# Linear attention into a gated feed-forward block on one core: batch 0's exponentials row by row on ScalarE, two more maximum trees, chunk 0 in halves, and a new written-out order

## The chip, the core and the metric

The kernel runs on one core of a Trainium2 chip. Its engines run side by side: TensorE (PE in the profile, its weight loads PEld) multiplies matrices, VectorE (DVE) and ScalarE (ACT) work on elements, GpSimd (POOL) does slower element work and issues some of the loads, SyncE (SP) issues the other loads and all stores. The metric is the device time of the whole program in microseconds: before the change the median of three runs is 242.53 us, between 241.72 and 242.69.

## What is computed

`q`, `k`, `v` have the shape 8 batches x 8 heads x 576 rows x 64, in float32. The feed-forward part has 4608 tokens (8 x 576) of width 512 and an inner width of 1024.

```python
q_s = softmax of q over the 64 features of a row          # + 1e-09 in the sum
k_s = softmax of k over the 576 rows, for each feature    # + 1e-09 in the sum
kv  = k_s^T @ v                 # 64 x 64 for each batch and head
x   = q_s @ kv                  # laid out as 4608 x 512
a, b = x @ w1, x @ w2           # 4608 x 1024 each
out = (a * b @ w3) @ w_out      # 4608 x 512, float32
```

## The kernel before

**Folding the weights.** `w3 @ w_out` is computed once, because the second part is linear after `a * b`. For each of eight slices `ft` of 128 rows of `w3`, step `w3t.ft` transposes the slice on PE (L416), `w3T.ft` copies it out of PSUM, `pf.ft.0` and `pf.ft.1` (L428) multiply it with the two halves of `w_out`, and `W3O.ft` scales it out. The loads are named `w3.0` to `w3.5` (the last two, `w3.4` and `w3.5`, hold two slices each: slices 4, 5 and 6, 7) and `wo.0`, `wo.1`.

**Attention of a batch `b`.** The 576 rows of a head lie as 64 partitions x 9 rows, two groups of heads fill the 128 partitions.
- For `k`: `kmx` is the maximum over the 9 rows that a partition holds. Batches below `TREES` (L285, two of them) take it as a tree of four `tensor_tensor` maxima over the whole tile (L469 to L472); the others as two `tensor_reduce` over half of the heads each (L460). `cb` (L474 to L488) brings it over the partitions: a transpose, reductions, a transpose back. `ksub` subtracts (L491), `kexp` takes the exponential on ScalarE (L499), `kv` multiplies with `v` on PE (L516, L526), `kv2` divides by the sum (L535 to L538).
- For `q`, in two parts (part 0 has 4, part 1 has 5 of a partition's 9 rows for each head): `qmx` maximum (L545), `qsub` subtraction (L550), `qexp` one exponential over the part (L558), `qsm` sum of each row (L563), `qeps` and `qrc` the reciprocal (L569, L575), `qn` the product (L582). Then `q` is transposed: on PE for batches 0 and 1 (`qt` L597, copied by `qT`), with a transposing DMA (`qd`) afterwards.
- `xm` and `xt` (L630) form `x` transposed, `xs` and `xts` scale it into SBUF as float16.

**Feed-forward of a chunk `c`.** Chunks 0 to 7 are 512 tokens of a batch each; chunk 8 gathers the last 64 tokens of all batches. For each slice `u`, `up.1` and `up.0` multiply with `w2` and `w1` (L744), `bs` copies the first out of PSUM, `ab` multiplies the two on VectorE (L759). `down.c.tb` (L766) sums eight matmuls, one for each slice of `ab`, for 128 tokens; `os` copies, `st` stores. A chunk in `SPLIT` (L294, chunk 1) is done in two halves of 256 tokens, named `sub` 0 and 1: a step `up.1.c.sub.u` then does two slices for half of the tokens. `down.c.0` reads the last `ab` of its half only in its last matmul, or in its last two where the chunk is split (two slices each).

**What sets the order.** All steps are written out in one list, `ORDER` (L80). Each engine gets its steps in that order and runs them strictly one after the other, so a step that waits holds up everything that is behind it on its engine. `PICKS` says which engine takes a step that two can do. `FILL` puts matmuls on zeros in front (17 at the start, 16 ahead of `pf.4.0`); nobody uses their result. For the first `LINKED` = 191 steps a step that holds the SBUF port that VectorE and GpSimd share waits for the last such step of the other engine (L71 to L75). `HW` (L193) are the loads that SyncE issues first, `LOADS` (L198) those of GpSimd; a GpSimd load also waits for the load eight places ahead of it to land (L401). The later loads are issued by SyncE, in the order of `ORDER`.

Of the kernel before, what the change touches and what calls it, by code (L numbers as in the profile page):

```python
# [17 lines left out]
class Plan:  # L18
# [8 lines left out]
    @staticmethod  # L27
    def group(name):

        if name[0] == "cast":  # L30
            return "_".join(str(x) for x in name)
        return f"{name[0]}_{min(name[1], 3)}_" + "_".join(str(x) for x in name[2:])
# [57 lines left out]
qT.1.0 up.1.0.0.3 ksub.1.0 ab.0.0.2 up.0.0.0.3 bs.0.0.3 kmx.2.1 kexp.1.1 xt.0 up.1.0.0.4 xts.0.1  # L90
up.0.0.0.4 xts.0.0 q.1.1 kexp.1.0 ab.0.0.3 up.1.0.0.5 cb.2 up.0.0.0.5 bs.0.0.5 bs.0.0.4 kv.1 q.2
W3O.6 v.2 ab.0.0.4 k.3 ksub.2.1 up.1.0.0.6 kv2.1 up.0.0.0.6 bs.0.0.6 ab.0.0.5 xm.1.0 up.1.0.0.7
ab.0.0.6 xs.1.0.0 ksub.2.0 xs.1.0.1 kexp.2.1 up.0.0.0.7 qmx.1.1 up.1.1.0.0 bs.0.0.7 up.0.1.0.0
ab.0.0.7 qsub.1.1 kexp.2.0 qmx.2.1 up.1.1.0.1 bs.1.0.0 up.0.1.0.1 bs.1.0.1 ab.1.0.0 up.1.1.0.2
qsub.2.1 qexp.1.1 qmx.2.0 down.0.0 q.3 qsm.1.1 v.3 vc.2.1 up.0.1.0.2 qexp.2.1 ab.1.0.1 up.1.1.0.3
vc.2.0 bs.1.0.2 qeps.1.1 os.0.0 up.0.1.0.3 qrc.1.1 bs.1.0.3 qsm.2.1 st.0.0 qn.1.1 kv.2 down.0.1
k.4 kv2.2 ab.1.0.2 qsub.2.0 qt.1.16 qt.1.8 ab.1.0.3 qT.1.16 down.0.2 qT.1.8 os.0.1 qmx.3.1
qexp.2.0 xm.1.1 down.0.3 xs.1.1.1 q.4 qsm.2.0 qsub.3.1 qeps.2.1 xs.1.1.0 qmx.3.0 os.0.2
up.1.1.1.0 os.0.3 up.0.1.1.0 qrc.2.1 bs.1.1.0 st.0.3 kmx.3.1 qn.2.1 qeps.2.0 xt.1 up.1.1.1.1
qexp.3.1 up.0.1.1.1 bs.1.1.1 qrc.2.0 qsm.3.1 down.1.0 xts.1.0 qn.2.0 qd.2.1 vc.3.1 ab.1.1.0  # L100
st.0.1 qeps.3.1 up.1.1.1.2 xts.1.1 qsub.3.0 qmx.4.1 qd.2.0 up.0.1.1.2 bs.1.1.2 vc.3.0 up.1.1.1.3
ab.1.1.1 qsub.4.1 v.4 ab.1.1.2 down.1.1 st.0.2 qexp.3.0 kmx.3.0 bs.1.1.3 up.0.1.1.3 os.1.0 os.1.1
st.1.0 xm.2.0 ab.1.1.3 down.1.2 xs.2.0.0 qrc.3.1 st.1.1 xs.2.0.1 cb.3 qn.3.1 xm.2.1 down.1.3
xs.2.1.1 xs.2.1.0 qsm.3.0 ksub.3.1 qd.3.1 qexp.4.1 up.1.2.0.0 kmx.4.0 up.0.2.0.0 bs.2.0.0 os.1.3
up.1.2.0.1 ksub.3.0 qeps.3.0 ab.2.0.0 up.0.2.0.1 bs.2.0.1 qsm.4.1 kexp.3.1 up.1.2.0.2 up.0.2.0.2
bs.2.0.2 qrc.3.0 ab.2.0.1 qn.3.0 kexp.3.0 up.1.2.0.3 ab.2.0.2 up.0.2.0.3 kmx.4.1 bs.2.0.3 kv.3
qd.3.0 up.1.2.0.4 k.5 ab.2.0.3 up.0.2.0.4 st.1.3 bs.2.0.4 kv2.3 os.1.2 up.1.2.0.5 ab.2.0.4 st.1.2
up.0.2.0.5 bs.2.0.5 qmx.4.0 xt.2 q.5 xm.3.1 xts.2.0 up.1.2.0.6 v.5 xts.2.1 ab.2.0.5 qsub.4.0
xs.3.1.1 xm.3.0 bs.2.0.6 xt.3 up.0.2.0.6 xts.3.1 xs.3.0.0 cb.4 up.1.2.0.7 xts.3.0 xs.3.0.1
up.0.2.0.7 xs.3.1.0 bs.2.0.7 ab.2.0.6 up.1.3.0.0 ksub.4.0 qexp.4.0 ab.2.0.7 down.2.0 kmx.5.1  # L110
bs.3.0.0 down.2.1 ksub.4.1 kexp.4.0 qmx.5.1 up.0.3.0.0 os.2.0 up.1.3.0.1 qsub.5.1 kexp.4.1
ab.3.0.0 down.2.2 qmx.5.0 bs.3.0.1 k.6 vc.4.1 kmx.5.0 qsub.5.0 up.0.3.0.1 qeps.4.1 up.1.3.0.2
vc.4.0 up.0.3.0.2 qrc.4.1 os.2.1 ab.3.0.1 qn.4.1 up.1.3.0.3 vc.5.0 qsm.4.0 st.2.1 down.2.3
# [12 lines left out]
up.0.5.0.0 qsm.6.0 qsub.7.0 down.4.0 qsm.6.1 down.4.1 os.4.0 qmx.7.1 kexp.6.0 up.1.5.0.1 bs.5.0.0
qeps.6.1 up.0.5.0.1 bs.5.0.1 qrc.6.1 ab.5.0.0 qn.6.1 up.1.5.0.2 ab.5.0.1 down.4.2 bs.5.0.2
kmx.7.1 qeps.6.0 qexp.7.0 qd.6.1 up.0.5.0.2 os.4.1 qrc.6.0 kv.6 ab.5.0.2 qn.6.0 xt.5 up.1.5.0.3
qsm.7.0 xts.5.0 os.4.2 up.0.5.0.3 xts.5.1 kmx.7.0 qsub.7.1 bs.5.0.3 qd.6.0 up.1.5.0.4 up.0.5.0.4
st.4.1 bs.5.0.4 ab.5.0.3 up.1.5.0.5 v.7 ab.5.0.4 st.4.0 up.0.5.0.5 bs.5.0.5 kv2.6 up.1.5.0.6  # L130
st.4.2 ab.5.0.5 xm.6.0 bs.5.0.6 xm.6.1 st.3.3 xt.6 up.0.5.0.6 xs.6.1.1 cb.7 xts.6.1 xts.6.0
up.1.5.0.7 xs.6.1.0 xs.6.0.0 up.0.5.0.7 xs.6.0.1 ab.5.0.6 down.4.3 ksub.7.1 qexp.7.1 bs.5.0.7
ab.5.0.7 up.1.6.0.0 os.4.3 qsm.7.1 vc.7.1 down.5.0 ksub.7.0 bs.6.0.0 qeps.7.1 up.0.6.0.0 qrc.7.1
up.1.6.0.1 ab.6.0.0 kexp.7.0 down.5.1 os.5.0 qeps.7.0 st.5.0 kexp.7.1 qrc.7.0 up.0.6.0.1 qn.7.0
st.4.3 vc.7.0 up.1.6.0.2 up.0.6.0.2 bs.6.0.1 qn.7.1 qd.7.0 bs.6.0.2 kv.7 up.1.6.0.3 ab.6.0.2
kv2.7 down.5.2 qd.7.1 ab.6.0.1 up.0.6.0.3 os.5.2 bs.6.0.3 up.1.6.0.4 st.5.2 ab.6.0.3 up.0.6.0.4
bs.6.0.4 up.1.6.0.5 ab.6.0.4 up.0.6.0.5 bs.6.0.5 os.5.1 up.1.6.0.6 ab.6.0.5 st.5.1 up.0.6.0.6
bs.6.0.6 xm.7.0 ab.6.0.6 xm.7.1 xs.7.0.0 xt.7 up.1.6.0.7 xs.7.1.1 up.0.6.0.7 xs.7.1.0 bs.6.0.7
xs.7.0.1 ab.6.0.7 down.6.0 xts.7.1 xts.7.0 up.1.7.0.0 os.6.0 up.0.7.0.0 st.6.0 up.1.7.0.1
up.0.7.0.1 bs.7.0.1 bs.7.0.0 down.6.1 up.1.7.0.2 os.6.1 down.5.3 bs.7.0.2 down.6.2 ab.7.0.1  # L140
ab.7.0.0 up.0.7.0.2 up.1.7.0.3 ab.7.0.2 up.0.7.0.3 bs.7.0.3 os.6.2 up.1.7.0.4 ab.7.0.3 up.0.7.0.4
bs.7.0.4 up.1.7.0.5 ab.7.0.4 up.0.7.0.5 bs.7.0.5 os.5.3 up.1.7.0.6 up.0.7.0.6 bs.7.0.6 ab.7.0.5
up.1.7.0.7 ab.7.0.6 up.0.7.0.7 bs.7.0.7 up.1.8.0.0 ab.7.0.7 down.7.0 bs.8.0.0 down.6.3 os.7.0
st.7.0 up.0.8.0.0 st.6.1 up.1.8.0.1 ab.8.0.0 st.6.2 up.0.8.0.1 bs.8.0.1 up.1.8.0.2 ab.8.0.1
up.0.8.0.2 os.6.3 bs.8.0.2 up.1.8.0.3 ab.8.0.2 up.0.8.0.3 bs.8.0.3 up.1.8.0.4 ab.8.0.3 up.0.8.0.4
bs.8.0.4 up.1.8.0.5 ab.8.0.4 down.7.1 bs.8.0.5 up.0.8.0.5 os.7.1 up.1.8.0.6 st.7.1 ab.8.0.5
up.0.8.0.6 bs.8.0.6 st.5.3 down.7.2 ab.8.0.6 st.6.3 up.1.8.0.7 up.0.8.0.7 os.7.2 bs.8.0.7 st.7.2
down.7.3 ab.8.0.7 down.8.0 os.7.3 st.7.3 down.8.1 os.8.0 st.8.0 down.8.2 os.8.1 st.8.1 down.8.3.0
os.8.2 down.8.3 st.8.2 os.8.3.0 st.8.3.0 os.8.3 st.8.3
"""  # L150


FILL = {
    "begin": 17, "pf.4.0": 16,
}


# [33 lines left out]


HW = [  # L193
    ("q", 0, 1), ("q", 0, 0),
]


# [8 lines left out]
def kernel(  # L206
# [75 lines left out]
    EVICT = 100.0  # L282
    SLACK = 0.0
    NX = 3
    TREES = 2  # L285
    DMATS = 1
    VCASTS = 2
    LEAD = [60.0, 30.0, 18.0]
# [53 lines left out]
    def side(name):  # L342
# [22 lines left out]
        if len(name) > 2:  # L365
            cut = slice(PARTS[name[2]][0] * D, PARTS[name[2]][1] * D)
# [518 lines left out]
```

## Time and profile before

| what | value |
| --- | --- |
| median of three runs | 242.53 us (241.72 to 242.69) |
| span of the profiled execution, first to last instruction | 240.1 us |
| what lies around that span, against the median | 2.4 us |
| PE, DVE, ACT, POOL busy | 231.1, 166.8, 129.4, 116.9 us |
| PE work on zeros (33 matmuls, L326) | 9.0 us |
| first matmul on data (`w3t`, L416) | at 8.87 us |
| `kv` of batch 0 (L516) | at 25.69 us |
| first `up` (L744) | at 34.84 us (its weight load) |
| last matmul ends | about 236.8 us |

The profile's page lists the busy time of each engine, groups of instructions by line, DMA queues, and the chain of work that ended last, followed back from the end. Three further views of the trace are used: the chain in order of time, the timeline (instructions by start time, with their duration and, in brackets, the idle time before and what ended it), and the groups by form. The trace also records when each load landed: the loads ahead of `v.0` land one after the other, and both queues share the same engines. Among them `q.0.1` landed at 5.06 us, `q.0.0` at 6.54, `w3.4` at 8.82, `k.0` at 11.82, `wo.0` at 14.15, `wo.1` at 16.57, `w3.3` at 17.82, `w3.0` at 19.13, `w3.1` at 20.38, `q.1.0` at 21.82, `v.0` at 25.56, then `w3.5` at 27.82, `w3.2` at 29.05, `w1.0` at 30.4, `k.1` at 33.55, `w2.0` at 34.75 and `k.2` at 37.64.

A duration in the trace runs from an instruction's start to its result. Where two VectorE instructions follow each other at once, the second starts a little before the first one's result; the distance of their starts is called the interval below (an `ab` has a duration of 0.68 and an interval of 0.60 us).

### The profile page before, as it was taken

Reading aid. Unit: us, or ns where it says so; the run is one execution under the profiler, and the core shown is the slowest. Engines: PE = TensorE matmul, PEld = TensorE weight load, DVE = VectorE, ACT = ScalarE, POOL = GpSimd, SP = SyncE. Lnnn points to the kernel's source line nnn. Section 1 sums busy time; section 2 is a strip of 40 time slices with the busy share of each in tenths; the row PEclk is TensorE's granted clock in tenths of the full one; section 3 lists DMA queues with packets and bytes.
Section 4 is the critical chain, followed back from the end, with each engine's and each line's share of the span. In section 5 each row is a group of like instructions: output and inputs, shape, how many; then the busy total and the mean of one; then the engine's idle time right before and its main releaser. Section 6 shows DMA issues by size and latency. Waiting matters only on the chain.

```text
span 240.1 us, 4806 instructions
## 1 busy us (share of the span) xinstructions
PE 231.1 (96%) x1917; PEld 114.7 (48%) x1917; DVE 166.8 (69%) x281; ACT 129.4 (54%) x211; POOL 116.9 (49%) x74
## 2 busy tenths in 40 slices
PE   7679899999999999999999999999999999999994
PEld 2336644457566444444544444444444444444442
DVE  2799789988998989988789879898244123523410
ACT  1358454855587784677468856638825414132121
POOL 8563745597989691698327784736620000000000
PEclk9999999999999999999999999999999999999999
DMA  6999999999999947967998780486273100050543
GB/s 206 311 209 253 244 359 203 216 344 373 400 363 194 288 96 180 387 204 240 206 387 133 157 327 0 57 181 237 68 125 85 44 0 3 0 131 0 132 132 131
DMA packets 37894, 45.66 MB, mean 190 GB/s; under 512 B 15984, under 2 KB 22384, under 8 KB 37872
## 3 DMA queue, kind: packets, MB, share of 16 engines
q1 hardware_dynamic: 30080, 34.22, 49.8%
q0 software_dynamic: 7792, 11.14, 21.2%
q8 instruction: 15, 0.25, 0.4%
q14 instruction: 7, 0.06, 0.1%
HBM read 38.80 MB, written 9.44 MB: 201 GB/s over the span
## 4 chain that ended last, share of the span: by engine, by line
PE 82%; DMA 10%; issue 2%; POOL 2%; DVE 1%; ACT 0%; DVEq 0%; POOLq 0%; ACTq 0%
PE pab L744 48%; PE po L766 22%; DMA v<-in_v_dram 7%; DMA q<-in_q_dram 3%; PE po L781 3%; PE po L428 3%; PE pkv L516 2%; PE xm L630 1%; POOL w L378 1%; PE w3t L416 1%; PE qtp L597 1%; DVE qr L563 1%; DVE qm L545 1%; PE po L630 1%; DVE ab L759 0%
## 5 line engine op out<-in xcount | busy, mean ns | idle before, releaser
L759 DVE TENSOR_TENSOR ab<-pab,bsb 128x512 f16<-128x512 f32 x72 | 48.5, 681 | 37.0 <-PE pab L744 25.5
L744 PE MATMUL pab<-x,w1sb 128*128 128x512 f16 (+1 forms) x288 | 65.8, 355 | 0.2 <-DVE ab L759 0.2
L744 PE MATMUL pab<-x,w2sb 128*128 128x512 f16 (+1 forms) x288 | 65.9, 356 | 0.0
L766 PE MATMUL po<-W3O,ab 128*128 128x512 f16 x256 | 59.7, 379 | 0.0
L299 ACT CAST bsb<-pab 128x512 f16<-128x512 f32 x58 | 33.7, 584 | 41.7 <-PE pab L744 38.3
L491 POOL TENSOR_TENSOR k<-k,cb 128x1152 f32<-128x1152 f32 x14 | 36.6, 2632 | 20.0 <-DVE cb L487 13.2
L744 PEld LDWEIGHTS <-w1sb 128*128 128x128 f16 x320 | 31.0, 98 | 30.9 <-issue 0.3
L744 PEld LDWEIGHTS <-w2sb 128*128 128x128 f16 x320 | 30.4, 98 | 30.1 <-issue 0.8
L582 POOL TENSOR_TENSOR en<-eq,qr 128x1280 f16<-128x1280 f16 (+1 forms) x15 | 32.0, 2141 | 22.6 <-DVE qr L575 22.6
L766 PEld LDWEIGHTS <-ab 128*128 128x128 f16 x256 | 24.7, 98 | 29.1 <-issue 0.7
L550 POOL TENSOR_TENSOR q<-q,qm 128x1024 f32<-128x1024 f32 (+1 forms) x14 | 29.7, 2126 | 10.8 <-DVE qm L545 9.6
L299 ACT COPY osb<-po 128x512 f32<-128x512 f32 (+1 forms) x33 | 19.1, 579 | 25.4 <-PE po L766 18.0
L545 DVE TENSOR_REDUCE qm<-q 128x20 f32<-128x1280 f32 (+1 forms) x16 | 21.5, 1343 | 8.1 <-DMA q<-in_q_dram 8.1
L460 DVE TENSOR_REDUCE km<-k 128x128 f32<-128x1152 f32 x12 | 25.8, 2159 | 0.0
L558 ACT ACTIVATE eq<-q 128x1280 f16<-128x1280 f32 (+1 forms) x16 | 18.7, 1167 | 8.0 <-POOL q L550 4.7
L563 DVE TENSOR_REDUCE qr<-eq 128x20 f32<-128x1280 f16 (+1 forms) x16 | 21.3, 1337 | 1.3 <-ACT eq L558 1.2
L499 ACT ACTIVATE ek<-k 128x1152 f16<-128x1152 f32 x16 | 18.6, 1161 | 4.1 <-POOL k L491 4.0
L428 PE MATMUL po<-wosb,w3T 128*128 128x512 f16 x64 | 15.5, 379 | 1.2 <-DMA wosb<-in_moe_w_out_dram 1.2
L303 ACT ACTIVATE x<-xm 128x512 f16<-128x512 f32 x21 | 12.0, 604 | 7.0 <-PE xm L630 6.8
L299 DVE CAST bsb<-pab 128x512 f16<-128x512 f32 x14 | 9.6, 687 | 6.5 <-PE pab L744 6.1
L299 ACT CAST v<-v 128x1152 f16<-128x1152 f32 x10 | 11.6, 1156 | 0.0
L326 PE MATMUL po<-zero 128*128 128x512 f16 x33 | 9.0, 435 | 1.6 <-DVE zero L321 1.6
(67 smaller groups left out, 172.0 us busy)
## 6 DMA issues: line engine op xcount, KB each, us to landing
out_dram<-osb SPq DMA_DIRECT2D x66, 128.0 KB, 2.5
q<-in_q_dram SPq DMA_DIRECT2D x6, 1152.0 KB, 7.8
v<-in_v_dram SPq DMA_DIRECT2D x6, 1152.0 KB, 10.0
k<-in_k_dram SPq DMA_DIRECT2D x5, 1152.0 KB, 7.6
k<-in_k_dram POOLq DMA_DIRECT2D x3, 1152.0 KB, 10.0
v<-in_v_dram POOLq DMA_DIRECT2D x2, 576.0 KB, 15.4
w<-in_moe_w_dram POOLq DMA_DIRECT2D x2, 512.0 KB, 11.6
wosb<-in_moe_w_out_dram POOLq DMA_DIRECT2D x2, 512.0 KB, 12.2
```

What stands on the lines that cost most here:

```text
L299: return [(nc.scalar.copy if eng == "ACT" else engine[eng].tensor_copy)(out=out, in_=in_)]
L428: nc.tensor.matmul(st["pf", ft], lhsT=st["w3T", ft][:, gt, :], rhs=wosb[:, gt, :], start=(gt == 0), stop=(gt == N_FT - 1))
L460: dve.tensor_reduce(out=st["km", b][:, two(hp), :], in_=kb[:, two(hp), :, :].rearrange("p h j d -> p h d j"), axis=AX.X, op=ALU.max)
L491: return [engine[eng].tensor_tensor(out=kb[:, two(hp), :, :], in0=kb[:, two(hp), :, :], in1=st["cb", b][:, two(hp), None, :].broadcast_to( ...
L545: dve.tensor_reduce(out=st["qm", b][:, :, j], in_=qb[:, :, j, :], axis=AX.X, op=ALU.max)
L550: return [engine[eng].tensor_tensor(out=qb[:, :, j, :], in0=qb[:, :, j, :], in1=st["qm", b][:, :, j, None].broadcast_to([P, HH, n, D]), op ...
L558: nc.scalar.activation(out=st["eq", b, p], in_=qb[:, :, j, :], func=AF.Exp)
L563: dve.tensor_reduce(out=st["qr", b][:, :, slice(*PARTS[p])], in_=st["eq", b, p], axis=AX.X, op=ALU.add)
L582: return [engine[eng].tensor_tensor(out=st["en", b][:, j, :, :].rearrange("p j h d -> p h j d"), in0=st["eq", b, p], in1=st["qr", b][:, :, ...
L744: nc.tensor.matmul(st["p", one, c, sub, u][:, a * (t1 - t0):(a + 1) * (t1 - t0)], lhsT=w[:, ct, fb * P:(fb + 1) * P], rhs=x()[:, ct, t0:t1 ...
L759: dve.tensor_tensor(out=st["ab", c][:, nf * u:nf * u + nf, t0:t1], in0=cut(st["p", 0, c, sub, u]), in1=cut(st["bsb", c, sub, u]), op=ALU.mult)
L766: nc.tensor.matmul(st["po", c, tb], lhsT=st["ab", c][:, ft, tb * P:(tb + 1) * P], rhs=W3O[:, ft, :], start=(ft == 0), stop=(ft == N_FT - 1))
```

## The change

- **Batch 0's q on ScalarE alone.** `QACT` names both parts of batch 0. `qmx` writes the negated maximum; `qexp` becomes one activation for each head and row (20 in part 1, 16 in part 0; 64 elements per partition), with the negated maximum as bias and the row's sum as accumulated output. `qsub` and `qsm` of batch 0 are gone.
- **q of batch 0 in four loads** on SyncE's queue, `q.0.part.half of the heads`, and `qmx` of batch 0 in four.
- **Trees for k in batches 2 and 3** (`TREES` 4): one step `kmx.b.0` instead of two.
- **Chunk 0 in halves** (`SPLIT` is [0, 1]): 128 matmuls over 256 tokens instead of 64 over 512.
- **A new order**, with picks for each step by itself, `LINKED` 350, 6 instead of 16 matmuls on zeros ahead of `pf.4.0`. GpSimd's loads change places: `w3.5`, `w3.2` now stand ahead of `v.0`, `k.0` behind the weights `wo` and `w3.3`, `w3.1`. `LATE` writes out the order of the later loads.

The diff, cut. Of the order, the new lines around the steps that are spoken of:

```diff
-LINKED = 191
+LINKED = 350
 ORDER
+q.0.1.1 q.0.1.0 q.0.0.1 qmx.0.1.1 qmx.0.1.0 w3.4 wo.0 wo.1 w3.3 w3.1 q.0.0.0 ident w3t.5 qexp.0.1
+w3T.5 w3t.4 w3T.4 pf.4.0 pf.5.0 pf.5.1 w3t.3 w3T.3 k.0 pf.4.1 W3O.4 qeps.0.1 qrc.0.1 W3O.5 w3.0
+qmx.0.0.1 w3.5 qmx.0.0.0 w3.2 qn.0.1 q.1.0 qt.0.16 w3t.1 w3T.1 qexp.0.0 qT.0.16 qeps.0.0 pf.3.0
+pf.3.1 W3O.3 pf.1.0 pf.1.1 kmx.0.0 qt.0.8 w3t.0 qT.0.8 w3T.0 v.0 k.1 w3t.7 W3O.1 w3t.6 w3T.7 qrc.0.0
+qn.0.0 w2.0 w1.0 w2.1 w1.1 pf.0.0 qt.0.0 pf.7.0 pf.0.1 w3t.2 pf.7.1 cb.0 ksub.0.0 kexp.0.0 ksub.0.1
+kexp.0.1 qmx.1.0 W3O.7 W3O.0 w3T.2 qT.0.0 w3T.6 kv.0 kv2.0 qsub.1.0 pf.2.0 pf.6.0 xm.0.0 pf.2.1
+pf.6.1 qexp.1.0 qsm.1.0 qeps.1.0 k.2 w2.2 w1.2 w2.3 kmx.1.0 qrc.1.0 w1.3 cb.1 xs.0.0.0 xs.0.0.1
+xm.0.1 xs.0.1.1 xs.0.1.0 up.1.0.0.0 up.0.0.0.0 up.1.0.1.0 up.0.0.1.0 bs.0.0.0 up.1.0.0.1 v.1 qn.1.0
+ksub.1.1 q.1.1 bs.0.1.0 ab.0.0.0 W3O.2 bs.0.0.1 qt.1.0 ab.0.1.0 W3O.6 up.0.0.0.1 ab.0.0.1 qT.1.0
+up.1.0.1.1 up.0.0.1.1 xt.0 up.1.0.0.2 up.0.0.0.2 kmx.2.0 ksub.1.0 bs.0.1.1 ab.0.1.1 xts.0.0 bs.0.0.2
+ab.0.0.2 xts.0.1 kexp.1.1 up.1.0.1.2 bs.0.1.2 up.0.0.1.2 up.1.0.0.3 up.0.0.0.3 cb.2 ab.0.1.2
+ksub.2.0 ksub.2.1 q.2 bs.0.0.3 kexp.1.0 ab.0.0.3 down.0.0 kv.1 kv2.1 up.1.0.1.3 up.0.0.1.3 xm.1.0
...
+xs.2.0.0 xs.2.0.1 qsm.3.0 qexp.3.1 qsm.3.1 xm.2.1 xs.2.1.1 qeps.3.0 qrc.3.0 ab.1.1.3 kmx.4.1
+down.1.2 st.0.1 st.0.2 q.5 xs.2.1.0 up.1.2.0.0 vc.3.1 bs.2.0.0 up.0.2.0.0 up.1.2.0.1 up.0.2.0.1
...
+kexp.5.0 ab.3.0.6 xm.4.0 up.1.3.0.7 kmx.6.1 bs.3.0.7 xs.4.0.1 xs.4.0.0 cb.6 kexp.5.1 up.0.3.0.7
+ab.3.0.7 down.3.0 os.3.0 up.1.4.0.0 bs.4.0.0 up.0.4.0.0 ab.4.0.0 qmx.7.0 up.1.4.0.1 bs.4.0.1
...
-    "begin": 17, "pf.4.0": 16,
+    "begin": 17, "pf.4.0": 6,
 HW
-    ("q", 0, 1), ("q", 0, 0),
+    ("q", 0, 1, 1), ("q", 0, 1, 0), ("q", 0, 0, 1), ("q", 0, 0, 0),
 LOADS
-    ("w3", 4), ("k", 0), ("wo", 0), ("wo", 1), ("w3", 3), ("w3", 0), ("w3", 1), ("q", 1, 0),
-    ("v", 0), ("w3", 5), ("w3", 2), ("w1", 0), ("k", 1), ("w2", 0), ("k", 2), ("w2", 1),
-    ("w1", 1), ("w2", 2), ("w1", 2), ("v", 1), ("w2", 3), ("w1", 3), ("q", 1, 1),
+    ("w3", 4), ("wo", 0), ("wo", 1), ("w3", 3), ("w3", 1), ("k", 0), ("w3", 0), ("w3", 5),
+    ("w3", 2), ("q", 1, 0), ("v", 0), ("k", 1), ("w2", 0), ("w1", 0), ("w2", 1), ("w1", 1),
+    ("k", 2), ("w2", 2), ("w1", 2), ("w2", 3), ("w1", 3), ("v", 1), ("q", 1, 1),
...
-    TREES = 2
+    TREES = 4
-    SPLIT = [1]
+    SPLIT = [0, 1]
+    QACT = [(0, 0), (0, 1)]
 qmx
-            dve.tensor_reduce(out=st["qm", b][:, :, j], in_=qb[:, :, j, :], axis=AX.X, op=ALU.max)
+            dve.tensor_reduce(out=st["qm", b][:, h, j], in_=qb[:, h, j, :], axis=AX.X, op=ALU.max,
+                              negate=True if (b, p) in QACT else None)
 qexp
+            if (b, p) in QACT:
+                if ("qr", b) not in st:
+                    st["qr", b] = work.tile([P, HH, NJ], F32, tag="qr", name="qr")
+                for h in range(HH):
+                    for x in range(*PARTS[p]):
+                        nc.scalar.activation(
+                            out=st["eq", b, p][:, h, x - PARTS[p][0], :], in_=qb[:, h, x, :],
+                            func=AF.Exp, bias=st["qm", b][:, h, x:x + 1],
+                            accum_out=st["qr", b][:, h, x:x + 1])
+                return
```

## The prediction

> **What bounds the kernel now.** I read the page's busy times first, then the chain that ended last, in order of time.
>
> ```profile
> span 240.1 us, 4806 instructions
> PE 231.1 (96%) x1917; PEld 114.7 (48%) x1917; DVE 166.8 (69%) x281; ACT 129.4 (54%) x211; POOL 116.9 (49%) x74
> PE 82%; DMA 10%; issue 2%; POOL 2%; DVE 1%; ACT 0%; DVEq 0%; POOLq 0%; ACTq 0%
> ```
>
> PE carries the chain; DVE's 69% is an average, so I look where PE was not the last.
>
> ```profile
> 9.10 16.45 DMA v<-in_v_dram
> 25.56 0.14 issue
> 25.69 0.77 PE pkv L516 x72
> 26.47 0.54 PE pkv L526 x36
> ...
> 56.59 0.32 DVE ab L759
> 56.91 0.28 issue
> 57.19 1.21 DVE qm L545
> 58.39 1.39 DVE qr L563
> 59.78 0.61 DVE ab L759
> 60.39 0.04 issue
> 60.44 1.03 PE pab L744 x8
> ```
>
> There are two places. Until 25.69 the front waits for loads, `v.0` last. Shortly before 60.44 the chain runs through DVE: it is just in time. After 60.44 the chain is PE's without a gap to 236.8, so before the change DVE never costs PE more there. What the change can win lies in the front; what it can lose is DVE's lead over PE. DVE's steps, from the timeline (start, duration):
>
> ```profile
> 33.57 1.22 DVE L469 TENSOR_TENSOR kmx<-k 128x1024 f32<-128x1024 f32 x1 [0.57 <-DMA k<-in_k_dram]
> 36.47 0.45 DVE L476 STREAM_TRANSPOSE kmq<-km 128x256 f32<-128x256 f32 x1
> 38.67 0.65 DVE L759 TENSOR_TENSOR ab<-pab,bsb 128x512 f16<-128x512 f32 x1
> 40.24 2.18 DVE L460 TENSOR_REDUCE km<-k 128x128 f32<-128x1152 f32 x1
> 42.33 0.69 DVE L759 TENSOR_TENSOR ab<-pab,bsb 128x512 f16<-128x512 f32 x1
> 42.93 2.16 DVE L460 TENSOR_REDUCE km<-k 128x128 f32<-128x1152 f32 x1
> ```
>
> From start to start: a tree 2.90 us, a `cb` 2.20, half of an untreed maximum 2.09, an `ab` 0.60. As medians over the trace, where instructions follow at once, I use tree 2.85, `cb` 2.17, `kmx` half 2.08, `ab`, `xs`, `W3O` and `os` 0.60, `bs` 0.61, `qmx` and `qsm` 1.40 or 1.13, `ksub` 1.27, `kv2` 0.89, `qrc` 0.19, `xts` 0.20.
>
> **Method.** I walk through the changed instruction lists engine by engine, each in its order, with these intervals, the waits of the code and the loads in the order of their queue. Done the same way, the kernel before ends at 237.7 instead of 240.1 us and starts `kv.0` at 25.3 instead of 25.7. So I add differences to the profiled execution: 240.1 us of span, and 2.4 us around it to the median of 242.53.
>
> **Part 1: the loads ahead of `kv.0`.** Ahead of `v.0` now stand `w3.5` and `w3.2` too. Before, exactly this set had landed when `w3.2` landed, at 29.05, and the queue was never empty. So `v.0` lands at about 29.05 and `kv.0` starts at 29.2: **+3.5 us**. PE then has less left: before, behind `kv.0` came three `w3t` (0.50 each), `qt.0.0` (0.45) and seven half folds `pf` (0.86 each); after it come four half folds. The three, the one and three halves, 1.50 + 0.45 + 2.59 = **-4.5 us**, move into the wait. They fit: when `w3.5` is there (22.7), PE has two `w3t`, `pf.0`, `qt.0.0`, `pf.7` and a last `w3t` to do, 5.4 us, done by 28.3. Moving `wo` ahead of `k.0` only shifts PE work inside this wait. The ten fewer matmuls on zeros (0.22 each) stood in waits for loads: nothing.
>
> **Part 2: halves of chunk 0.** In the chain, chunk 1's 16 matmuls over 256 tokens take 1.75 us where 8 over 512 take 1.73; eight such groups give **+0.1**.
>
> **Part 3: singles on ScalarE.** No row has 64 elements with an accumulated sum. Nearest is `qeps` (L569), 20 elements with a bias from SBUF: 0.31 us, start to start 0.21. With 44 elements more at 0.86 ns (the difference of the 1280 and 1024 element exponentials, 1.28 and 1.06) that is 0.25 us. Below, `kexp`'s interval of 1.07 for 1152 elements leaves 0.14 for 64; above, if the sum costs a second instruction of such length, 0.5. I take 0.25, the nearest row: 5.0 us for part 1, 4.0 for part 0, from 6.4 (behind the 1.28 us table load) to 11.4, and from about 17. They lie beside PE's wait for loads, and DVE saves `qsub.0.1` and two `qsm`, about 3.9 us, but also in the wait. In the walk 0.14 and 0.25 cost **nothing**; from 0.3 on it costs, because `w3T` and `W3O` copies stand behind the 16 singles and PE waits for them: 0.35 gives +1.5, 0.5 gives +5.2. [...]
>
> **Part 4: trees.** 2.85 instead of two times 2.08 saves DVE 1.3 us in batch 2 and in batch 3. But `LINKED` makes GpSimd's `ksub.1.0` wait for the tree of batch 2 (2.8 us in the walk); `kv.1` stands behind `down.0.0`, late anyway (part 5), and that hides it. Without that cover it would delay `kv.1` by up to 2.8.
>
> **Part 5: the order on DVE.** The new list does DVE's k and q work earlier, ahead of the `ab` that a `down` on PE ends with. I count what stands in each queue from `kv2.0` on DVE and from `kv.0` on PE.
> - To `ab.0.0.3`, which `down.0.0` needs: `kv2`, `qsm`, two trees, `qrc`, two `cb`, seven `ab`, two `W3O`, `xts`, `bs`, `ksub` = 0.89 + 1.13 + 5.69 + 0.19 + 4.33 + 4.19 + 1.20 + 0.20 + 0.61 + 1.27 = 19.7 us. PE ahead of `down.0.0`: `kv.0` 1.31, four half folds 3.46, two `xm` 0.68, 14 `up` 12.2, `qt` and `xt` 0.63 = 18.3. DVE starts when `kv.0` is done, 1.5 us after PE, and idles 0.4 us in between: in the walk `ab.0.0.3` is ready at 50.7, while PE reaches `down.0.0` at 47.4 and could do six of eight matmuls (1.3 us): **2.1 us lost**.
> - To `ab.1.1.3`, for `down.1.2`: DVE 48.3 us, PE 48.5 plus the loss so far. `qsm.3.0` and `qsm.3.1` stand just ahead. Ready at 82.1, wanted at 81.2: with a small wait at `down.1.0`, **1.2 us lost**.
> - To `ab.3.0.7`, for `down.3.0`: DVE 90.2 us, PE 89.4. `kmx.6.1` (2.08) and `cb.6` (2.17) stand just ahead of that `ab`. Ready at 125.6, wanted at 123.2: **2.4 us lost**.
>
> Before the change the same counts to chunk 3 are 84.7 us on DVE and 93.8 on PE: a lead of 9.1 us for DVE becomes none. Later DVE leads again (126.0 against 134.5 to `ab.5.0.7`), and PE runs through. Losses: 2.1 + 1.2 + 2.4 = **+5.7**. Against it stands one wait of the walk before, `up.0.0.0.6` for `w1.3`, which goes (the load now lands at about 45.5, ahead of need): **-0.4**. What is late next there is `w2.3` and `w1.3` themselves, without loss. Stores and late loads on SyncE end no wait of PE in the walk, though `st.0.0` stands behind `k.4`.
>
> **Sum.** 3.5 - 4.5 + 0.1 + 0 + 5.7 - 0.4 = +4.4, about +4.3 in the walk with its own `kv.0`. The span becomes 244.4, the time **246.8 us**, 1.8% slower.
>
> **Rivals.**
> 1. *DVE keeps pace, not slower.* The relief (two trees, no `qsub` and `qsm` in batch 0) could count for more than the order. For it: the chain of before shows DVE late only once, by 0.17 us at 60.44. The mechanism is that `ab.0.0.3`, `ab.1.1.3` and `ab.3.0.7` are ready before PE asks. Then the 5.7 go and 3.5 - 4.5 + 0.1 - 0.4 = -1.3 is left: 241.2 us. It decides when DVE does its 19.7 us to `ab.0.0.3` in 17.6, 11% less than the rows. Against it: the rows are steady. If only a part of the losses shows, some 1.3 of 5.7, the time is that of before.
> 2. *The singles are dear.* Accumulating costs a second instruction: at 0.35 us each +5.8 in all (248.3), at 0.5 us +9.5 (252.0). For it: no row has the operation. Against: the interval of `qeps`, and that one instruction is listed for each.
> 3. *The change does not do what it says*: the loads do not land in the order of the list, because two queues share the engines; `v.0` lands earlier or later by some 1.3 us (one 0.5 MB load). The time moves less than that, since DVE starts from `kv2.0` as well: 245.5 to 248.
> 4. *The clock.* Longer gaps could lower PE's granted clock; the page's row of it shows nines throughout, with gaps up to 1.9 us ahead of the first `w3t`. Three losses at half clock for a few us each would give 249 to 252. [...]
>
> **Chances.** Forecast (with rival 3) 0.58, own range 244.6 to 248.8; singles dear 0.15; clock 0.04; DVE keeps pace wholly 0.10, in part (241.5 to 243.7) 0.13. A measurement of this kernel can tell about 0.5%, 1.2 us, from no change. Faster by more 0.10, within 0.14, slower 0.76. The range leaves out the whole of rival 1 below and the dearest singles above: 242.6 to 250.4.
>
> **What would show it.** Right: `kv` of batch 0 at about 29.2, the first `up` at about 35, PE waiting for DVE `ab` (L806 of the changed kernel) by some 2 us near 49, 1 near 81, 2.4 near 123, and none after 130; singles about 0.25 us start to start. Wrong: `v.0` landing far from 29, no wait of PE for `ab`, or `w3T` copies late behind the singles. The prediction fails if DVE's intervals beside a busier ScalarE differ from before, or if the walk's idle times on DVE (5.8 us to `ab.3.0.7`) are not there: the counts alone give 30.6 + 90.2 = 120.8 on DVE against 29.1 + 89.4 + 1.5 = 120.0 on PE, 0.8 us lost in all, and 242.0 us.

## The result and the profile after

The changed kernel takes **250.28 us** (249.98 to 253.0, 4 executions) where the kernel before took 242.12 beside it: a ratio of 1.035 (95% interval 1.031 to 1.039), slower. Forecast was 246.8, with a range of its own from 244.6 to 248.8, so 8.2 us were lost and not 4.3. The profiled execution took 250.22 us with a span of 248.4. Six more executions, in a second run, moved the median of all ten only to 250.4. One execution of the kernel before, 246.11 us at a granted clock of 0.993, is left out of all comparisons below as a slow one.

The page after, the lines that answer to those of before:

```profile
span 248.4 us, 5022 instructions
PE 231.7 (93%) x1979; PEld 120.0 (48%) x1979; DVE 179.1 (72%) x316; ACT 123.8 (50%) x249; POOL 112.5 (45%) x73
PE 79%; DVE 7%; DMA 6%; ACT 4%; issue 2%; POOL 1%; DVEq 0%; POOLq 0%
PEclk9999999999999999999999999999999999999999
```

PE's busy time is what it was (231.7 for 231.1), and the span is 8.3 longer: in this execution, whose clock is 1.00 to the last matmul, all of the loss is PE waiting. DVE's share of the chain rose from 1 to 7%, and ScalarE has a share of 4% that it did not have. The chain in order of time shows where (start, duration, what):

```profile
3.21 14.32 DMA w<-in_moe_w_dram
...
20.34 5.31 ACT eq L593 x32
26.14 0.75 issue
26.88 1.05 ACT w3T L323
27.97 1.04 PE po L455 x4
...
53.35 1.34 DVE k L519
54.69 0.61 DVE ab L806
55.35 0.60 PE po L813 x2
...
83.60 2.54 DVE qr L603 x2
86.30 0.56 DVE ab L806
86.90 0.60 PE po L813 x2
...
126.16 2.10 DVE km L488
128.28 0.46 DVE kmq L504
128.76 0.43 DVE mx L507
130.48 0.66 DVE ab L806
131.18 0.39 PE po L813
```

Three times DVE comes last just ahead of a `down`, behind the very steps that the prediction named: `ksub.2.0`, the two `qsm.3`, `kmx.6.1` and `cb.6`. From the end of one matmul's issue to the next, PE waits there 2.03, 0.66 and 2.30 us, 5.0 in all (5.7 forecast), and never after 131. The other half lies in the front, where a load and then the singles (L593) come last. The first `up` starts at 39.05 us (35.05 before, about 35 forecast). 4.0 in the front and 5.0 at the downs, less 0.33 for the old wait at 60 that went, is 8.7; the last matmul of the `down` line (L813, L766 before) starts 8.5 later (237.98 for 229.48).

The groups by form show what a single is:

```profile
L593 ACT ACTIVATE eq<-q,qm 128x64 f16<-128x64 f32 x36 | 12.0, 346 | 0.0
L593 ACT ACTIVATION_READ_ACCUMULATOR eq<-q,qm 128x1 f32 x36 | 7.2, 199 | 0.0
```

The sum is a second instruction of 0.199 us. From one single to the next it is 0.332 us, not 0.25. And the list of loads (source, queue, count, KB each, median us from issue to landing) shows that the last two of q's four take 13.2 us in the median (11.2 and 15.1 in the trace):

```profile
q<-in_q_dram SPq DMA_DIRECT2D x2, 320.0 KB, 3.4
...
q<-in_q_dram SPq DMA_DIRECT2D x2, 256.0 KB, 13.2
```

`q.0.0.0` lands at 17.35 us where the whole `q.0.0` had landed at 6.54, and `w3.5`, forecast at 22.7, at 25.31.

### The profile page after: what moved, and what is told of

Read it like the earlier page. It is cut to its first block, busy times and chain, and to the rows that moved or that the text cites. A ratio compares the mean times of both kernels' runs of the same rounds, so it can differ in the third digit from the quotient of the medians.

```text
span 248.4 us, 5022 instructions
## 1 busy us (share of the span) xinstructions
PE 231.7 (93%) x1979; PEld 120.0 (48%) x1979; DVE 179.1 (72%) x316; ACT 123.8 (50%) x249; POOL 112.5 (45%) x73
## 4 chain that ended last, share of the span: by engine, by line
PE 79%; DVE 7%; DMA 6%; ACT 4%; issue 2%; POOL 1%; DVEq 0%; POOLq 0%
PE pab L791 47%; PE po L813 20%; DMA w<-in_moe_w_dram 6%; PE po L455 3%; PE po L828 3%; ACT eq L593 2%; PE pkv L544 2%; DVE ab L806 2%; PE xm L670 1%; ACT w3T L323 1%; DVE qr L603 1%; DVE km L488 1%; ACT W3O L327 1%; PE po L670 1%; PE qtp L637 1%
## 5 line engine op out<-in xcount | busy, mean ns | idle before, releaser
L813 PE MATMUL po<-W3O,ab 128*128 128x512 f16 x256 | 60.4, 379 | 4.5 <-DVE ab L806 4.5
L813 PEld LDWEIGHTS <-ab 128*128 128x128 f16 x256 | 24.2, 98 | 34.3 <-DVE ab L806 6.0
L519 POOL TENSOR_TENSOR k<-k,cb 128x1152 f32<-128x1152 f32 x12 | 31.4, 2626 | 15.9 <-issue 7.2
L323 ACT COPY osb<-po 128x512 f32<-128x512 f32 (+1 forms) x22 | 12.5, 567 | 27.9 <-PE po L813 19.9
L574 DVE TENSOR_REDUCE qm<-q 128x16 f32<-128x1024 f32 (+3 forms) x18 | 21.4, 1204 | 5.9 <-DMA q<-in_q_dram 5.9
L323 DVE COPY osb<-po 128x512 f32<-128x512 f32 x15 | 10.4, 690 | 15.4 <-PE po L813 11.4
L603 DVE TENSOR_REDUCE qr<-eq 128x16 f32<-128x1024 f16 (+1 forms) x14 | 18.7, 1338 | 1.0 <-ACT eq L598 0.9
L488 DVE TENSOR_REDUCE km<-k 128x128 f32<-128x1152 f32 x8 | 17.1, 2142 | 0.0
L598 ACT ACTIVATE eq<-q 128x1024 f16<-128x1024 f32 (+1 forms) x14 | 16.2, 1168 | 0.5 <-POOL q L580 0.5
L323 DVE CAST bsb<-pab 128x512 f16<-128x512 f32 x20 | 13.8, 688 | 3.5 <-PE pab L791 3.2
L593 ACT ACTIVATE eq<-q,qm 128x64 f16<-128x64 f32 x36 | 12.0, 346 | 0.0
L455 PEld LDWEIGHTS <-w3T 128*128 128x128 f16 x64 | 5.8, 98 | 10.4 <-ACT w3T L323 2.0
```

The costliest lines, as they stand in the source:

```text
L323: return [(nc.scalar.copy if eng == "ACT" else engine[eng].tensor_copy)(out=out, in_=in_)]
L455: nc.tensor.matmul(st["pf", ft], lhsT=st["w3T", ft][:, gt, :], rhs=wosb[:, gt, :], start=(gt == 0), stop=(gt == N_FT - 1))
L488: dve.tensor_reduce(out=st["km", b][:, two(hp), :], in_=kb[:, two(hp), :, :].rearrange("p h j d -> p h d j"), axis=AX.X, op=ALU.max)
L519: return [engine[eng].tensor_tensor(out=kb[:, two(hp), :, :], in0=kb[:, two(hp), :, :], in1=st["cb", b][:, two(hp), None, :].broadcast_to( ...
L574: dve.tensor_reduce(out=st["qm", b][:, h, j], in_=qb[:, h, j, :], axis=AX.X, op=ALU.max, negate=True if (b, p) in QACT else None)
L603: dve.tensor_reduce(out=st["qr", b][:, :, slice(*PARTS[p])], in_=st["eq", b, p], axis=AX.X, op=ALU.add)
```

## The experiments

**Theories.** *A*: late loads, because the four loads of q share the engines with GpSimd's list, cost the front up to 3 us; the singles' sums cost 1.2 more; the order on DVE costs what the waits at the downs show. *B*: the singles cause nearly all of the front's loss. *C*: nothing waits for them. *D*: DVE has no room, and waits taken away at the downs come back elsewhere. After the first four runs came *E*: waits of PE of about 2 us lower its granted clock, and the time at half clock is part of the loss; *F*: the clock falls for another reason. "Clock" is the mean granted clock of an execution; 0.007 less is 3.4 us at half clock, 1.7 us of lost time.

**1. `a_two_loads`**: the changed kernel, q of batch 0 in two loads.

```diff
-    ("q", 0, 1, 1), ("q", 0, 1, 0), ("q", 0, 0, 1), ("q", 0, 0, 0),
+    ("q", 0, 1), ("q", 0, 0),
```

> The changed kernel with q of batch 0 in two loads again (qmx of each part whole); singles, order, trees and halves stay. Theory A (loads): the second pair of q's loads shares the DMA engines with GpSimd's list until 17.35 us and pushes that list back. Then q.0.0 lands near 6.5 us instead of 17.35, w3.4 near 8.8 instead of 10.26, v.0 near 29.1 instead of 30.63, kv.0 starts near 31 instead of 32.6, and the time is 1.5 to 3 us under the changed kernel's 250.3: about 248. Rival B (singles): PE waits in the front for ScalarE, not for loads: the loads land earlier, kv.0 stays at 32 to 32.6, time 249.8 to 250.3.

250.52 us (249.69 to 251.53), ratio 1.034 (1.026 to 1.042): no gain. Yet the loads came as theory A says: `q.0.0` at 6.74, `w3.5` at 23.05, `v.0` at 29.00, first `up` at 36.70, 2.35 us sooner than in the profiled execution of the changed kernel. All but 0.7 of that was lost again by 86 us: in this execution the clock was 0.50 between 53.6 and 57 us, behind PE's wait at `down.0.0`. All four executions had a clock of 0.986 or 0.993. Both A's price and B fall, and E was formed.

**2. `a_three_loads`**: `q.0.1` in two loads, `q.0.0` whole.

```diff
+    ("q", 0, 1, 1), ("q", 0, 1, 0), ("q", 0, 0),
```

> The changed kernel with q.0.1 still in two loads and q.0.0 whole (three issues on SyncE, the last near 1.74 us instead of 1.24 before the change). Theory A in its form 'what SyncE's queue has not moved when GpSimd's list starts near 4 us goes at a tenth of the rate': q.0.0 lands late, 12 to 17 us, and the time is near the changed kernel's, 249.5 to 250.3. Theory A in its form 'it is the halving of q.0.0': q.0.0 lands near 7 and the time is that of two loads, 247.5 to 248.8. Rival B: 249.8 to 250.3 with q.0.0 near 7.

250.97 us (two executions, clock 0.986). `q.0.0` landed at 15.29, 13.5 us after its issue. So it is not the halving: what SyncE issued third, near 1.74 us, came late beside GpSimd's list; what it issued second, near 1.24, did not (`q.0.0` at 6.74 us in run 1).

**3. `a_no_sums`**: no accumulators.

```diff
+                    dve.memset(st["qr", b], 64.0)
...
-                            accum_out=st["qr", b][:, h, x:x + 1])
```

> The changed kernel without the row sums: the 36 single ACTIVATEs of batch 0 have their bias but no accumulator, and the sums are a constant written by DVE, so batch 0 is not normalised (the output is not the reference's). Theory A: the accumulator read is the difference between the forecast 0.25 us and the measured 0.332 us from single to single; without it they start every 0.24 to 0.27 us, ScalarE is free 1.6 us earlier near 11 us and 1.3 us earlier near 25 us, and the time falls by about 1.2 us, to 249.0 (248.7 to 249.4). Rival B (the singles cause nearly all of the front's loss): 246.5 to 247.5. Rival C (nothing waits for ScalarE there): 250.0 to 250.5.

249.38 us (248.04 to 251.04). On the timeline eight singles follow each other without a read:

```profile
6.15 2.02 ACT L594 ACTIVATE eq<-q,qm 128x64 f16<-128x64 f32 x8
```

That is 0.24 us from start to start, close to the forecast's 0.25, without the sum. From `w3.5`'s landing (26.09) to the first `up` (38.56) it is 12.5 us, where the changed kernel, in both profiles, and `a_two_loads` need 13.7: the sums cost 1.2 us in the front there. That agrees with A, against B and C; the times (0.9 below the changed kernel's, overlapping) do not settle it alone.

**4. `a_ab_first`**: DVE's order altered in three places.

```diff
-... up.0.0.0.3 cb.2 ab.0.1.2 ksub.2.0 ksub.2.1 q.2 bs.0.0.3 kexp.1.0 ab.0.0.3
+... up.0.0.0.3 ab.0.1.2 q.2 bs.0.0.3 kexp.1.0 ab.0.0.3 cb.2 ksub.2.0 ksub.2.1
-... qsm.3.0 qexp.3.1 qsm.3.1 ... qrc.3.0 ab.1.1.3
+... ab.1.1.3 qsm.3.0 qexp.3.1 qsm.3.1 ... qrc.3.0
-... bs.3.0.7 xs.4.0.1 xs.4.0.0 cb.6 kexp.5.1 up.0.3.0.7 ab.3.0.7
+... xs.4.0.1 xs.4.0.0 up.0.3.0.7 bs.3.0.7 ab.3.0.7 cb.6 kexp.5.1
```

> The changed kernel with DVE's order altered in three places: cb.2 and both ksub.2 behind ab.0.0.3; ab.1.1.3 ahead of the two qsm.3; up.0.3.0.7, bs.3.0.7 and ab.3.0.7 ahead of cb.6. Theory A (PE waits at three downs for an ab queued behind attention work): the waits of 2.03 us before down.0.0 and 0.66 us before down.1.2 go, the one of 2.30 us before down.3.0 falls to about 0.7, some 1.0 us comes back near 59 and 68 us (xm.1.0 on kv2.1, kv.2 on vc.2.1): 3.4 us less, 246.9 (246.0 to 247.8). Rival D (DVE has no room between 45 and 130 us, so the same time reappears at the next product): 249.5 to 250.3.

**245.75 us** (244.82 to 247.21), ratio 1.014 (1.006 to 1.021). The group of `down` matmuls, with PE's idle time ahead of them behind the bar, in the changed kernel:

```profile
L813 PE MATMUL po<-W3O,ab 128*128 128x512 f16 x256 | 60.4, 379 | 4.5 <-DVE ab L806 4.5
```

and here:

```profile
L814 PE MATMUL po<-W3O,ab 128*128 128x512 f16 x256 | 60.2, 379 | 0.6 <-DVE ab L807 0.4
```

The waits left are 0.51 us near 55, 0.32 near 66 and 0.56 near 126, close to what was expected. Theory D falls. The gain of 4.5 us is over the 3.4 expected, and in three of four executions the clock was 0.998 or more.

**5. `c_after_again`**: the changed kernel, nothing altered.

> The changed kernel once more, as it is, for what its executions have in common: theory E says that its times are a time at full clock (about 248.0: two of the four executions so far give it, with about 1.7 us added for each 0.007 by which the mean granted clock is below 1) plus stretches of some 3.4 us at half clock after PE's waits of 2 us, which the kernel before does not have. Then most executions show a mean clock of 0.98 to 0.993 and the median is 249.5 to 250.5. Theory A (late loads instead): the time does not go with the clock.

251.01 us (250.26 to 253.34, six executions), 0.5 above the expected range. With the first run, nine of ten executions of the changed kernel have a clock of 0.98 to 0.993; those of before that are compared have 0.998 to 1.000. In this profile the clock falls twice, behind two waits: 2.09 us of waiting for `w3.5` (to 24.2 us), 0.50 from 24.7 to 28.1; and 2.03 us at `down.0.0` (to 54.2), 0.50 from 55.4 to 58.8. Behind 2.30 us at `down.3.0` it stays 1.00 here, as in every profile. The times alone do not follow the clock (253.34 at 0.98, but 250.26 at 0.993 and, in the first run, 250.22 at 1.0 with late loads).

**6. `c_fill`**: 8 matmuls of zeros in each of two waits.

```diff
-    "begin": 17, "pf.4.0": 6,
+    "begin": 17, "pf.4.0": 6, "down.0.0": 8, "down.3.0": 8,
```

> The changed kernel with 8 matmuls of zeros (about 1.7 us of PE) put ahead of down.0.0 and of down.3.0 each, into PE's waits of 2.03 and 2.30 us for ab.0.0.3 and ab.3.0.7; they use a free PSUM buffer and nothing else changes. Theory E: more work for PE and less time: the stretch at half clock that follows the first wait no longer comes, mean clock 0.993 to 1.0 in most executions, median 248.0 to 249.0 beside 249.5 to 250.5 for the changed kernel on the same chip. Rival F (the clock falls for another reason, or in the front): the same share of executions with a lower clock, and the same median within 0.4.

250.22 us (250.01 to 251.09, five executions): less than `c_after_again` by 0.8, with overlapping intervals and above the 248.0 to 249.0 of theory E, so the time settles nothing. The profile does, for its place. Windows (stretch, us; busy time and count of PE, PEld, DVE, ACT, POOL; granted clock; DMA share; GB/s), first of `c_after_again`:

```profile
55.00:59.00 4.00, 4.00 (x114) 3.11 (x100) 2.29 (x6) 2.07 (x3) 1.69 (x2) 0.57 0.60 175
```

then of `c_fill`:

```profile
55.00:59.00 4.00, 4.00 (x136) 3.02 (x135) 2.38 (x7) 2.46 (x4) 1.73 (x2) 1.00 0.47 114
```

The stretch at half clock behind `down.0.0` is gone; one in the front, from 26 to 29.4 us behind a wait of 1.94 us for `w3.5`, is left, and the wait at `down.1.2` grew from 0.66 to 1.31 us.

**7. `c_b_singles`**: the kernel before with the singles alone.

```diff
+    QACT = [(0, 0), (0, 1)]
```

> The kernel before with ScalarE's singles alone (36 single ACTIVATEs with bias and accumulator for batch 0, no qsub.0 and no qsm.0); order, loads, trees and chunks as before. In that order w3T.3 and W3O stand behind the singles and pf.4.0 waits. With 0.332 us each, as measured: 3.6 us more than before, 245.7; with 0.25, as forecast: 0.6 more, 242.7. With PE's long wait near 13 to 20 us a stretch at half clock may add up to 1.7 (theory E).

247.17 us (two executions), 5.5 more than before: 3.6 for singles of 0.332 us and 1.7 for the clock were expected together. The clock is 0.985:

```profile
15.00:22.00 7.00, 2.22 (x6) 0.84 (x7) 2.62 (x11) 5.63 (x25) 2.76 (x2) 0.57 1.09 243
```

PE has 2.22 us of work in 7 there, because `w3T` stands behind the singles, and does most of that at half clock.

**8. `c_b_four`**: the kernel before with the four loads alone (`HW` as in the changed kernel, `qmx.0` in halves).

> The kernel before with the four loads of q of batch 0 alone (and qmx.0 of each part in halves). Theory A2 (the SyncE loads issued third and fourth are moved beside GpSimd's list): q.0.0.1 lands near 12 and q.0.0.0 near 16, where q.0.0 landed at 6.54; qmx.0.0 holds DVE and qsub.0.0 holds GpSimd until then, and the time is 244 to 250. Rival (the late landing needs the changed kernel's list): both by 8 us, time 242 to 242.5.

248.94 us (two executions, clock 0.979). `q.0.0.0` landed at 15.93: the late landing does not need the changed list, and the rival falls. In the old order DVE and GpSimd wait for it, PE goes idle, and the clock is 0.53 from 15 to 26 us. In the new order, where `q.0.0` is wanted later, run 1 could show no such cost.

**9. `d_ab_two`**: runs 1 and 4 together.

> The changed kernel with q of batch 0 in two loads and with DVE's order as in a_ab_first, nothing else altered (singles with sums, trees, halves stay). By the terms measured so far: w3.5 lands near 23.0, first up 36.6 to 36.7 (35.05 before the change), waits at the downs of 1.2 us in all, no wait of 2 us behind the front, so mostly full clock there: 244.0 to 244.7 (after 250.5, a_ab_first 245.75). If the second pair of loads costs nothing (rival to A): the same as a_ab_first, 245.7.

245.97 us (244.43 to 246.0), ratio 1.014 (1.008 to 1.019): as `a_ab_first`, so against A once more. But three executions, at a clock of 0.991 or 0.992, took 245.95 to 246.0, and one, at 0.999, took 244.43, the time expected. The profile shows the fall in the front, from 25.2 us, behind a wait of 2.11 us for `w3.5` (landed at 23.74); the first `up` starts at 37.91, 1.2 us later than expected.

**10. `d_all`**: runs 1, 3 and 4 together.

> d_ab_two without the row sums of batch 0 (the accumulators are left out, a constant stands for them, so batch 0 is not normalised and the output is not the reference's): all three terms that the forecast and the runs name are taken out, while trees, halves and the rest of the order stay. First up at 35.3 to 35.6, no wait of 1.5 us for w3T.0, and 1.2 us less than d_ab_two: 242.8 to 243.5, that is within 1.5 us of the kernel before (241.7). If it stays at 245 or above, a fourth cause is missing.

244.55 us (243.55 to 245.45, ten executions), ratio 1.010 (1.007 to 1.013). Five executions at 0.998 or more took 243.55 to 243.89, five at 0.993 or less 245.21 to 245.45. The first `up` started at 35.64. No large cause is missing: of the 1.6 us by which the profiled span (241.8, at full clock) lies above that of before (240.1), 0.6 is the front and 1.0 the remaining waits (0.50, 0.32 and 0.56, less the old 0.33).

**11. `d_b_trees`**: the kernel before with the trees alone.

```diff
-    TREES = 2
+    TREES = 4
-... ab.0.0.1 ... kmx.2.0 ... ab.0.0.2 ... kmx.2.1 ... ab.0.0.3        (and kmx.3.1)
+... ab.0.0.1 ... kmx.2.0 ... ab.0.0.2 ... ab.0.0.3
```

> The kernel before with the trees alone: kmx of batch 2 and 3 as four tensor_tensor instead of two reductions. DVE is busy 2.6 us less; the tree of batch 2 stands whole between ab.0.0.1 and ab.0.0.2, so PE waits some 0.85 us near 45 and 0.7 near 48: 242.2 to 243.0 (before 241.7). If a shorter DVE were worth its saving: 240.4 to 241.4.

246.55 us (246.05 to 246.96), ratio 1.017 (1.013 to 1.022): missed on the other side, and not by the clock (0.998 to 1.0). The timeline of GpSimd (start, duration, instruction; in brackets the idle time before and what ended it):

```profile
38.77 2.61 POOL L497 TENSOR_TENSOR k<-k,cb 128x1152 f32<-128x1152 f32 x1 [4.26 <-DVE cb L493]
41.34 0.78 POOL L383 DMA_DIRECT2D w1sb<-in_moe_w_dram  x1
44.38 2.62 POOL L497 TENSOR_TENSOR k<-k,cb 128x1152 f32<-128x1152 f32 x1 [2.26 <-DVE km L478]
46.94 0.78 POOL L383 DMA_DIRECT2D q<-in_q_dram  x1
```

and that of DVE between the two subtractions:

```profile
41.42 1.23 DVE L475 TENSOR_TENSOR kmx<-k 128x1024 f32<-128x1024 f32 x1 [1.41 <-POOL k L497]
42.68 0.69 DVE L476 TENSOR_TENSOR kmx<-kmx 128x512 f32<-128x512 f32 x1
```

In the code a tree is a step marked `port`, and the two `tensor_reduce` are not. So by `LINKED` it waits for one `ksub.1` on GpSimd and makes the next one wait 2.26 us; `q.1.1`, issued behind that `ksub`, lands only at 55.5. PE waits 1.56 us near 47 and 1.63 near 57, and about 1 us each near 84 and 109. The tree of batch 3, which is not linked, has a first step of 2.38 us beside a GpSimd subtraction where 1.23 is the same step's time in batch 2: the one measure here of what the code's port stands for.

**12. `d_b_halves`**: the kernel before with chunk 0 in halves alone.

```diff
-    SPLIT = [1]
+    SPLIT = [0, 1]
```

> The kernel before with chunk 0 in halves alone (64 up matmuls of 256 columns two by two in place of 512, in the places of the whole ones). As forecast, 0.02 us for each of 16 ups is 0.2 to 0.3 us at most: 241.7 to 242.2. Rival: 256-column matmuls cost half as much again per column: 244 or above.

242.66 us (241.74 to 243.29, ten executions), ratio 1.000 (0.997 to 1.003); the kernel before took 242.26 beside it. As forecast, nothing that can be told.

**13. `e_fill_front`**: `d_ab_two` with zeros in the wait for `w3.5`.

```diff
+            for i in range(9 if ft == 7 else 0):
+                nc.tensor.matmul(st["w3t", ft].rearrange("p a b -> p (a b)").bitcast(F32),
+                                 lhsT=zero[:, 0:P], rhs=zero, start=True, stop=True)
```

> d_ab_two (two loads, DVE's order altered) with 9 matmuls of zeros put ahead of w3t.7's transposes, into the same PSUM tile, where PE waits 2.1 us for the load w3.5 near 22 us. Theory E: PE's waits of 2 us are what lowers the clock; filled, the stretch at half clock near 25 to 28.5 us no longer comes, all executions have a mean clock of 0.998 or more, and the median falls from 245.97 to 244.0 to 244.6 although PE has more to do. Rival F (the clock falls in the front for another reason): three executions in four at 0.992 as in d_ab_two, median 245.7 to 246.3.

**244.59 us** (244.48 to 244.77, six executions), ratio 1.009 (1.006 to 1.012). All six are at 0.997 or more, within 0.3 us. The window without the zeros (`d_ab_two`):

```profile
25.00:29.00 4.00, 3.68 (x16) 1.93 (x17) 3.81 (x7) 3.17 (x5) 3.70 (x5) 0.57 1.15 289
```

and with them:

```profile
25.00:29.00 4.00, 3.73 (x31) 2.19 (x30) 3.81 (x7) 3.17 (x5) 3.76 (x5) 1.00 1.16 286
```

PE does 31 matmuls there instead of 16 in the same busy time. `w3.5` landed at 23.74 us without the zeros and at 23.84 with them, so the loads don't make the difference; the first `up` started at 36.45 and not at 37.91. The intervals of the two ratios overlap; what decides is that all six executions lie where only one of four lay without the zeros. More work made the kernel 1.4 us faster: E holds in the front, F does not.

**14. `e_fill_all`**: the changed kernel with zeros in all its waits of 2 us (run 6, and 7 matmuls ahead of `w3t.7`).

> The changed kernel with matmuls of zeros in all its waits of 2 us: 7 ahead of w3t.7, 8 ahead of down.0.0, 8 ahead of down.3.0; order, loads and singles stay. Theory E: mean clock 0.998 or more in most executions, median 248.0 to 248.8 (its time at full clock), that is 1.7 to 2.4 us below the changed kernel's 250.5 with the waits themselves still paid. Rival F: 250 to 251 with clocks of 0.98 to 0.993.

249.18 us (247.89 to 250.27, six executions), ratio 1.027 (1.023 to 1.032) beside 1.039 (1.034 to 1.044) for `c_after_again`. Five of six are at 0.999 or more: the clock is what E says. The time missed the forecast a little, because at that clock three executions took 247.89 to 248.3 and two 250.05 and 250.27. The profiled one, 250.19 us at 0.993, had `w3.5` at 25.36 and its first `up` at 38.98, as late as the changed kernel's first profile; whether late loads make the slower times was not settled.

No version beat the kernel before.

## Why the prediction was wrong in size

In the profiled execution the front and the waits at the `down`s give the whole 8.5 us: the first `up` came 4.0 us later where no delay was forecast (parts 1 and 3), and part 5's waits are as forecast. In nine of ten executions the clock fell as well (rival 4). By the prediction's own steps:

- **Part 5, the order on DVE: right.** Three waits of 2.03, 0.66 and 2.30 us, at the steps named, for 2.1, 1.2 and 2.4; the middle one is about half. Undoing the three moves took 4.5 us off the median.
- **Parts 2 and 4: right** for this kernel. Halves cost nothing alone (run 12), and PE waits for no tree. Run 11 agrees with part 4 that its cover matters: in the old order, without it, the two trees cost 4 us.
- **Rival 4, the clock, is the step that failed.** It was given a chance of 0.04, on the full clock of the profile before, with gaps of up to 1.9 us; that the gaps of part 5 would leave the clock alone was the author's estimate. The runs disagree: waits of 1.9 to 2.3 us were followed by some 3.4 us at a clock of 0.50, not in every execution and not at every place.

  In each profile the clock changes only at whole multiples of one step of 3.413 us, counted from the start of the trace's first clock record (in `c_after_again` at 4.19, 24.67, 28.09, 55.39 and 58.81 us: 0, 6, 7, 15 and 16 steps), and where the steps begin differs from execution to execution (that first record starts at 4.70 us before the change and at 6.29 in the changed kernel's first profile). The sixteen profiles hold 1032 such steps at full clock up to 230 us. In 14 of them PE was busy for at most 47% of the step: 12 were followed by a step at half clock, and none of the other 1018 was; the 47% is read off these same profiles. So in these profiles a wait of 2 us was dear where it lay in one step, and free of this where two steps shared it. `down.0.0` shows both: PE was busy for 45% of the step from 51.98 us in `c_after_again`, which was followed by the fall, and for 83 and 63% of the two steps that share the wait (from 50.67 and 54.08) in the changed kernel's first profile, which was not. The gap of 1.9 us before the change, on which the prediction leaned, was shared too (65% in the step from 4.70 us).

  The fall costs 1.4 us in the front (runs 9 and 13) and 1.2 to 1.8 in the changed kernel (median 250.4 of ten and 251.0 of six, against 249.2 with the waits filled; these stem from different chips). The rival's own price, 249 to 252, covers what was measured, but with three falls; the profiles show one or two. Falls don't simply add up: in `c_after_again` it is 13.7 us from `w3.5`'s landing to the first `up`, with the fall, as in the first profile without it, where PE waits 1.4 us for `w3T` instead. Each forecast wait was priced as its own length, and where the clock fell it cost more than that.
- **Part 3 failed in size.** A single costs 0.332 us and not 0.25, since the accumulator is read by an instruction of its own, of 0.199 us. The prediction said that from 0.3 on it costs and that `w3T` copies stand behind the 16 singles; the chain shows just that (5.31 us of `eq`, then `w3T`, then `pf.0.0`). Its walk had +1.5 at 0.35. It measured 1.2 us in the front (run 3), less where `w3.5` lands late against the singles (12.6 us from its landing to the first `up` with the sums in run 13, 12.05 without in run 10), and some 0.85 in time at full clock (244.59 in run 13 to 243.75, the median of the five in run 10). The nearest row, `qeps`, had no sum.
- **Part 1 failed in size.** `w3.5` landed at 23.7 to 26.1 us with three or four loads of q (median of seven profiles 24.3) and at 23.05 to 23.84 with two, for 22.7 forecast; in the profiled execution that is 2.6 us and nearly all that part 3 leaves of the front. `v.0`, forecast at 29.05, landed at 30.63 there and at 29.00 in run 1, so what failed is "They fit": behind `w3.5` PE still had the 5.4 us of work counted there, and a wait of about 1.5 for `w3T`, and `kv.0` started at 32.55 instead of 29.2 (at 30.20 in run 1). That q's last loads share with GpSimd's list is shown (runs 1, 2 and 8): the halves of a load that took 5.3 us before took 13.2 beside it. How the engines divide themselves between the two queues was not shown. What it costs in time was not found: runs 1 and 9 gave no gain in the median, and the clock covers it.

So the profiled execution lost its time to late loads at full clock; `c_after_again`, the other one with a trace, had earlier loads and a lower clock; and both end near 250. How often each comes stays open. Behind the longest wait, at `down.3.0`, the clock never fell: in four of the five profiles that have this wait, PE was busy for 48% or more of every step that it touches, but in the first profile only for 41% of the step from 129.17 us, and why no fall followed there stays open.

## What to carry to other kernels

Here a wait of PE of 2.1 us cost 1.4 us beyond its length, in one execution and not in the next (runs 9 and 13), so look at the granted clock behind each new wait, over several executions, before pricing it; where the wait can't go, try matmuls of zeros in it, which were cheaper than the wait alone (244.59 for 245.97 us). An accumulator on a 64-element activation was a second instruction of 0.199 us, and a row without it is no price for it. Two trees that save DVE 1.3 us each by the rows cost 4 us (run 11), where a linked `ksub` on GpSimd waited 2.26 us for one and the other's first step took 2.38 us for 1.23 beside a GpSimd subtraction; try a part alone in the old order before calling it a gain.

## What the runs showed of the hardware that was not expected

- Granted clock 0.50 for about 3.4 us, beginning 0.2 to 2.1 us after PE resumed from a wait of 1.9 to 2.3 us (in `a_no_sums` once from one of about 4 us); with 7 to 9 matmuls of zeros in that wait it stayed at 1.00. The changes lie on steps of 3.413 us, and 12 of the 14 steps in which PE was busy for at most 47% were followed by one at half clock.
- ACTIVATE over 64 elements with a bias: 0.24 us from start to start, with a sum 0.332.
- A load of 256 KB that SyncE issued third, while GpSimd's list ran, took 7.3 to 12.2 us from issue to landing, one issued fourth 12.0 to 15.8; those of 320 KB ahead of them took 3.1 to 3.6.
- The trace has 16 landings for one load, at different times: `w3.5`'s first at 22.2 to 23.1 us in all profiles of the changed kernel's order, its last 0.7 to 3.0 us later.
- `tensor_tensor` maximum of 1024 elements on DVE: 1.23 us alone, 2.38 beside a GpSimd subtraction (run 11, once).
